# Hash attention and a gated feed-forward on one core: attention steps re-timed, hash bits of both halves together, pair loads two pairs ahead

## The chip, the cores and the metric

The kernel runs on one core of one Trainium2 chip. The metric is the device time of one execution in microseconds (us), as a median over several executions. A profiled execution also gives a span, from the first to the last instruction of the core, and a trace of every instruction. Engines are named as the profile names them: PE (matmul), PEld (its weight loads), DVE (vector), ACT (scalar), POOL, and SP, which here only issues transfers; SPq, ACTq and POOLq are the instruction queues from which transfers are issued.

## The reference

Two blocks in sequence. The attention has 4 batches, 8 heads, 768 positions and head size 64; a query attends to the keys whose six hash bits equal its own. The feed-forward block takes the 3072 x 512 result through 512 x 2048 and 2048 x 512 weights.

```python
q_bits = (np.einsum('bhsd,dk->bhsk', q, proj) > 0).astype(np.int64)   # k_bits likewise
mask = q_bucket[:, :, :, None] == k_bucket[:, :, None, :]
scores = np.where(mask, scale * np.matmul(q, k.transpose(0, 1, 3, 2)), -1000000000.0)
attn = softmax(scores)            # with 1e-9 added to the sum
x = np.matmul(attn, v)            # (B,H,S,D) -> (B*S, H*D)
h = x @ w_in
g = h * erf(softplus(h))
out = g @ w_out
```

The two weight matrices come as 64-bit floats. The kernel turns each into 32-bit floats on the chip, in 16 pieces of 128 x 512 for each matrix.

## The kernel before, in words

**Attention.** Heads go in pairs: 16 pairs, the two heads of a pair in the two halves of the partitions. Each pair has four steps, so there are 64 steps n; pair i has the steps 4i to 4i+3. In the text r is n modulo 4. Steps 4i and 4i+1 serve the first half of the queries (384), 4i+2 and 4i+3 the second; the even step of a half takes the first 384 keys, the odd step the others. The order is written out by hand: inside `tc.manual_schedule()` each engine does its instructions in the order of the program, and waits where an operand is not there. A step consists of

- `scores(n)` on PE: three PSUM tiles `st` (pool tag `big`, three buffers of two banks), first from the bits in bf16, then from q and k in f32, so that pairs without equal bits are pushed far below zero;
- `exponentials(n)` on ACT: three `e` tiles of 128 x 768 (nine tiles in rotation);
- `sum_keys(n)` on DVE: adds the `e` tiles of a half into `sum`; the first addition of a half is L329, the other four are L332;
- `weigh(n)` on PE: `av` from `e` and v, one step later than the scores;
- `divisor(n)` on PE, once for each half, on the step behind its last one: it multiplies `sum` by ones (`z_ps`, L356), which sums over the keys;
- `leave(n)`: ACT copies `av` into `xT` and `z_ps` into `z`.

The hash bits of the next pair are made meanwhile, a quarter in each step: a matmul into a bank of its own (L191), then `take_bits`, on ACT for the bits of q (L197) and on DVE for those of k (L199).

The row of sums `z` is inverted and spread in three parts for each pair: `spread` (SP: `z` to memory as `zd`, and back as `zc`), `invert` (DVE: L398 and L401 on `zc`; SP: `rd<-zc`, then `r<-rd`, which broadcasts it over the partitions), and `normalise` (DVE: L417 multiplies `xT` by `r`). They stand at r = 0, r = 2 and r = 3 of the pair behind. At r = 0, ahead of everything else, SP is also given the six loads of q, k and v of the next pair (`fetch`).

The weights are converted between: `fetch_weights` (POOLq issues the transfer `raw`), `round_weights` part 0 in even steps (ACT: L250, L251; DVE: L254, L262), part 1 in odd ones (DVE: L274, L282, L285; POOL: L293 adds the two parts, `top` and `rest`).

**Feed-forward.** Units of 256 tokens by 512 hidden features; `hidden` (L567) and `project` (L645) on PE, the activation function on ACT and DVE between. Beside it `extremes` reads q and k again to get a bound on the scores, `judge` turns it into a flag, and a second, general form of the attention stands behind a branch on that flag.

The loop of the attention, from the program:

```python
scores(n)
taking = bits(i + 1, r) if i + 1 < NPAIR else None
if 1 <= n <= NS:
    sum_keys(n - 1); weigh(n - 1)
if n < NS:
    exponentials(n)
    if taking: taking()
if 1 <= n <= NS and (n - 1) % 2 == 1:
    divisor(n - 1); leave(n - 1)
```

Of the kernel before, what the change touches and what calls it, by code (L numbers as in the profile page):

```python
# [46 lines left out]
P = 128  # L47
# [16 lines left out]
def kernel(  # L64
# [32 lines left out]
    psum = ctx.enter_context(tc.tile_pool(name="psum", bufs=3, space=PSUM))  # L97
    proj_sb = const.tile([P, P], F32, name="proj_sb")
# [10 lines left out]
    for ab in range(2):  # L109
        for c in range(2):  # L110
            nc.sync.dma_start(
                out=proj_sb[ab * D : ab * D + D, ab * D + c * NBIT : ab * D + (c + 1) * NBIT],
                in_=proj2[ab * D : ab * D + D, ab * NBIT : (ab + 1) * NBIT],
            )
# [69 lines left out]
    def hash_bits(d, r, bitp):  # L184

        what, half = ("q", "q", "k", "k")[r], r % 2
        cols = slice(half * HS, (half + 1) * HS)
        if half == 0:
            d[what + "b"] = bitp.tile([P, S], BF16, name=what + "b", tag=what + "b")
        ps = bank("bits", 1)[:, 0:HS]  # L190
        nc.tensor.matmul(out=ps, lhsT=proj_sb, rhs=d[what][:, cols], start=True, stop=True)  # L191
        return what, cols, ps

    def take_bits(d, what, cols, ps):
        dst = d[what + "b"][:, cols]
        if what == "q":
            nc.scalar.activation(out=dst, in_=ps, func=AF.Sign, scale=2.0**100, bias=sgn[:, 0:1])  # L197
        else:
            nc.vector.tensor_scalar(  # L199
                out=dst,  # L200
                in0=ps,
# [6 lines left out]
    def attention():  # L208
        NS = NPAIR * 4
        with (  # L210
# [4 lines left out]
            tc.tile_pool(name="norm", bufs=1) as norm,  # L215
            tc.tile_pool(name="small", bufs=3) as small,
# [9 lines left out]
            def fetch_weights(n):  # L226
                if n >= len(pieces):
                    return
                if not WIDE:
                    nc.gpsimd.dma_start(out=pieces[n][0], in_=pieces[n][1])  # L230
                else:
                    raws[n] = rawp.tile([P, WP, 2], I32, name="raw", tag="raw")
                    nc.gpsimd.dma_start(
# [3 lines left out]
            def round_weights(n, part):  # L237
# [55 lines left out]
                nc.gpsimd.tensor_tensor(  # L293
# [30 lines left out]
            def sum_keys(n):  # L324
                d = pairs[n // 4]
                es = [etiles[(n * GC + c) % len(etiles)][:, :, 0:HS] for c in range(GC)]
                if n % 2 == 0:
                    d["sum"] = sums.tile([P, 2, HS], F32, name="sum", tag="sum")
                    nc.vector.tensor_tensor(out=d["sum"], in0=es[0], in1=es[1], op=ALU.add)  # L329
                    es = es[2:]  # L330
                for e in es:
                    nc.vector.tensor_tensor(out=d["sum"], in0=d["sum"], in1=e, op=ALU.add)  # L332
# [19 lines left out]
            def divisor(n):  # L352
                d = pairs[n // 4]
                z = d["z_ps"] = bank("z_ps", 1)[:, 0:HS]
                for ab in range(2):
# [3 lines left out]
                        rhs=d["sum"][:, ab, :],  # L359
                        start=True,  # L360
                        stop=True,
                    )

            def leave(n):
# [6 lines left out]
                if half == 0:  # L371
# [8 lines left out]
                    d["z"] = norm.tile([P, S], F32, name="z", tag="z")  # L380
                nc.scalar.copy(out=d["z"][:, cols], in_=d["z_ps"])
# [39 lines left out]
            def bits(i, r):  # L421
                what, cols, ps = hash_bits(pairs[i], r, bitp)
                return lambda: take_bits(pairs[i], what, cols, ps)

            for i in range(2):
                pairs[i] = fetch(i, load)
            for n in range(2):
                fetch_weights(n)
            for r in range(4):
                bits(0, r)()  # L430
            for n in range(NS + 4):
                i, r = divmod(n, 4)
                if n < NS:
                    if r == 0 and i >= 1 and i + 1 < NPAIR:
                        pairs[i + 1] = fetch(i + 1, load)
                    scores(n)
                    taking = bits(i + 1, r) if i + 1 < NPAIR else None
                if 1 <= n <= NS:
                    sum_keys(n - 1)
                    weigh(n - 1)  # L440
                if n < NS:
                    exponentials(n)
                    if taking:
# [339 lines left out]
```

## Time and profile before

| | |
|---|---|
| median of three executions | 1126.29 us (1125.39 to 1129.95) |
| profiled execution: its time / its span | 1128.4 us / 1126.5 us |
| PE busy | 1057.3 us, 94% of the span |
| DVE busy | 809.8 us, 72% |
| ACT busy | 678.0 us, 60% |
| POOL busy | 77.9 us, 7% |
| mean clock granted to PE | 0.983 of full speed |
| first scores (L308) / first feed-forward matmul (L567) | 17.95 us / 441.11 us from the start of the span |

The attention is the stretch between the last two times. In a row of the timeline the columns are start, duration, engine, line, operation and tiles, count, and in brackets the idle time of the engine ahead of it and what ended it. In a row of groups they are busy time and mean duration of one, and behind the last bar the idle time ahead of them with its releasers.

### The profile page before, as it was taken

How to read it: one execution, taken by the hardware profiler on the slowest of the kernel's cores; microseconds unless marked ns; L12 is line 12 of the kernel's file. 1: busy time of each engine (PE TensorE's matmuls, PEld its weight loads, DVE VectorE, ACT ScalarE, POOL GpSimd, SP SyncE). 2: the span in 40 equal slices, each digit the busy share in tenths (PEclk: the TensorE clock that was granted, in tenths of full speed). 3: DMA queues.
4: the chain of work that ended last, by engine and by line, in shares of the span. 5: the costliest groups of instructions: out<-in, count | busy, mean ns of one | idle time of the engine just before them, and what ended most of it. 6: DMA issues, size and time to landing. Idle time of an engine off the chain costs nothing.

```text
span 1126.5 us, 11846 instructions
## 1 busy us (share of the span) xinstructions
PE 1057.3 (94%) x4482; PEld 608.6 (54%) x4482; DVE 809.8 (72%) x962; ACT 678.0 (60%) x785; POOL 77.9 (7%) x68
## 2 busy tenths in 40 slices
PE   5999898999989987989999999999999998999987
PEld 2434333334334334856666666666666665666633
DVE  2767676767777773699787877777777767666692
ACT  3555555555555542597666666666666665666691
POOL 0211111111221120000000000000000000000000
PEclk9999999999999998999999999999999999999999
DMA  7133334434434311100101011111110000000000
GB/s 163 58 95 95 95 95 95 103 96 120 114 99 110 95 53 40 32 29 29 47 28 47 29 47 30 45 42 35 41 47 29 19 9 10 10 10 10 9 19 22
DMA packets 55329, 61.98 MB, mean 55 GB/s; under 512 B 33728, under 2 KB 41920, under 8 KB 55264
## 3 DMA queue, kind: packets, MB, share of 16 engines
q1 hardware_dynamic: 50512, 44.37, 15.6%
q0 software_dynamic: 4608, 16.78, 4.7%
q8 instruction: 37, 0.61, 0.2%
q14 instruction: 28, 0.23, 0.1%
q10 hardware_dynamic: 144, 0.00, 0.0%
HBM read 54.63 MB, written 6.49 MB: 54 GB/s over the span
## 4 chain that ended last, share of the span: by engine, by line
PE 75%; DVE 12%; DMA 8%; issue 2%; ACT 1%; SPq 1%; DVEq 0%
PE h_ps L567 28%; PE o_ps L645 28%; PE st L308 9%; PE av L344 6%; DMA r<-rd 5%; DVE sum L332 5%; PE bits L191 3%; DMA rd<-zc 2%; PE z_ps L356 2%; DVE xT L417 1%; DVE rest L285 1%; DVE top L274 1%; ACT xT L370 1%; SPq L408 1%; DVE unit L282 1%
## 5 line engine op out<-in xcount | busy, mean ns | idle before, releaser
L645 PE MATMUL o_ps<-w_out_sb,h 128*128 128x512 f32 x768 | 338.5, 595 | 7.5 <-DVE h L634 7.5
L567 PE MATMUL h_ps<-xT,w_in_sb 128*128 128x256 f32 x1536 | 342.6, 382 | 0.0
L567 PEld LDWEIGHTS h_ps<-xT,w_in_sb 128*128 128x128 f32 x1536 | 294.5, 192 | 59.1 <-issue 13.4
L645 PEld LDWEIGHTS o_ps<-w_out_sb,h 128*128 128x128 f32 x768 | 146.3, 191 | 175.0 <-issue 166.5
L320 ACT ACTIVATE e<-st 128x768 f32<-128x768 f32 x192 | 141.9, 809 | 92.0 <-PE st L308 89.2
L332 DVE TENSOR_TENSOR sum<-sum,e 128x768 f32<-128x768 f32 x128 | 150.7, 1177 | 9.3 <-DVE sum L332 0.5
L580 ACT COPY h<-h_ps 128x1024 f32<-128x1024 f32 x48 | 48.6, 1013 | 171.8 <-PE h_ps L567 162.8
L308 PE MATMUL st<-q,k 64*128 64x384 f32 x768 | 140.8, 501 | 0.0
L344 PE MATMUL av<-e,v 128*64 128x385 f32 (+1 forms) x768 | 137.9, 495 | 0.0
L626 DVE SCALAR_TENSOR_TENSOR s<-q,s 128x1024 f32<-128x1024 f32 x96 | 111.1, 1220 | 21.8 <-ACT q L625 21.8
L625 ACT ACTIVATE q<-z,cq 128x1024 f32<-128x1024 f32 x96 | 102.3, 1137 | 0.4 <-DVE s L608 0.4
L308 PEld LDWEIGHTS st<-q,k 64*128 64x128 f32 x768 | 75.6, 198 | 41.6 <-issue 6.6
L344 PEld LDWEIGHTS av<-e,v 128*64 128x64 f32 x768 | 49.5, 136 | 80.6 <-issue 71.7
L654 DVE COPY ob<-o_ps 128x512 f32<-128x512 f32 x24 | 16.4, 687 | 79.8 <-PE o_ps L645 79.8
L594 ACT ACTIVATE e<-e 128x1024 f32<-128x1024 f32 x48 | 49.1, 1046 | 35.2 <-DVE e L581 35.2
L356 PE MATMUL z_ps<-sum,ones 128*64 128x384 f32 x128 | 29.9, 545 | 36.8 <-DVE sum L332 36.8
L634 DVE TENSOR_TENSOR h<-h,s 128x1024 f32<-128x1024 f32 x48 | 56.6, 1220 | 7.1 <-ACT s L633 6.7
L598 DVE TENSOR_TENSOR w<-e,w 128x1024 f32<-128x1024 f32 x48 | 58.8, 1225 | 1.7
L608 DVE SCALAR_TENSOR_TENSOR s<-s,w 128x1024 f32<-128x1024 f32 x48 | 58.8, 1225 | 1.6
L605 DVE SCALAR_TENSOR_TENSOR s<-h,s 128x1024 f32<-128x1024 f32 x48 | 58.5, 1219 | 0.0
L626 DVE SCALAR_TENSOR_TENSOR s<-z,s 128x1024 f32<-128x1024 f32 x48 | 56.5, 1220 | 0.0
L667 DVE TENSOR_REDUCE most<-t 128x1 f32<-128x384 f32 x64 | 33.0, 549 | 31.6 <-DMA t<-in_qkT_dram 31.5
(57 smaller groups left out, 821.0 us busy)
## 6 DMA issues: line engine op xcount, KB each, us to landing
t<-in_qkT_dram SPq DMA_DIRECT2D x64, 192.0 KB, 2.4
raw<-in_w_in_dram POOLq DMA_DIRECT2D x16, 512.0 KB, 3.9
raw<-in_w_out_dram POOLq DMA_DIRECT2D x16, 512.0 KB, 3.8
q<-in_qkT_dram SPq DMA_DIRECT2D x32, 192.0 KB, 4.1
k<-in_qkT_dram SPq DMA_DIRECT2D x32, 192.0 KB, 6.9
v<-in_v_dram SPq DMA_DIRECT2D x32, 192.0 KB, 4.5
r<-rd SPq DMA_DIRECT2D x32, 192.0 KB, 3.2
out_dram<-ob SPq DMA_DIRECT2D x24, 256.0 KB, 2.0
```

The lines of the kernel that those rows point to most:

```text
L308: nc.tensor.matmul(out=d["st"][c][:, ab, 0:HS], lhsT=d["k" + src][rows, keys], rhs=d["q" + src][rows, cols], start=(part == 0), stop=(part ...
L320: nc.scalar.activation(out=e[:, :, 0:HS], in_=st[:, :, 0:HS], func=AF.Exp, scale=scale)
L332: nc.vector.tensor_tensor(out=d["sum"], in0=d["sum"], in1=e, op=ALU.add)
L344: nc.tensor.matmul(out=d["av"][rows, 0:w], lhsT=d["v"][:, g * GC + c, rows], rhs=e[:, ab, 0:w], start=(g == 0 and c == 0), stop=(g == 1 an ...
L567: nc.tensor.matmul(out=ps[:, f, :], lhsT=w_in_sb[:, kc, (g * G + f) * P : (g * G + f + 1) * P], rhs=xT[b][:, kc, t0 : t0 + T], start=(kc = ...
L598: nc.vector.tensor_tensor(out=w, in0=e, in1=w, op=ALU.subtract)
L605: nc.vector.scalar_tensor_tensor(out=s, in0=h, scalar=0.0, in1=s, op0=ALU.max, op1=ALU.add)
L608: nc.vector.scalar_tensor_tensor(out=s, in0=s, scalar=S_MAX, in1=w, op0=ALU.min, op1=ALU.add)
L625: nc.scalar.activation(out=q, in_=z, func=AF.Square, bias=cq[:, j : j + 1])
L626: nc.vector.scalar_tensor_tensor(out=s, in0=q, scalar=r, in1=s, op0=ALU.add, op1=ALU.mult)
L634: nc.vector.tensor_tensor(out=d["h"], in0=d["h"], in1=s, op=ALU.mult)
L645: nc.tensor.matmul(out=ps, lhsT=st[t * NG + f // G]["h"][:, f % G, tt * P : (tt + 1) * P], rhs=w_out_sb[:, f, :], start=(f == 0), stop=(f ...
```

## The change

1. `divisor` moves a step later: the one for the half that ended in step n-2 stands at the end of the odd step n, behind `weigh(n-1)`; each half has a `sum` tile of its own in the pair's record, and the copy of `z_ps` moves along. `leave` stays at the even steps.
2. `spread` goes from r = 0 to r = 1, `invert` from r = 2 to r = 3, and `normalise` from r = 3 to r = 1 of the pair after that.
3. The addition that ends a piece of weights moves from POOL to DVE.
4. The bits of both halves are made at once: q at r = 0, k at r = 2, in one tile of the tag `big` instead of the single bank, and taken by one instruction of 768 elements instead of two of 384.
5. The loads of pair i+2 are issued at r = 1 of pair i (before: pair i+1 at r = 0 of pair i).
6. At the start the four small loads of `proj_sb` go to ACT's queue, and the first two pieces of weights to SP's queue, behind the loads of pair 0.
7. Behind step 64 the rest of the last two pairs' work is done in the first three rounds of the feed-forward (`late`), where `normalise(14)`, the last `divisor` and `spread(15)`, `invert(15)` and `normalise(15)` stand behind a `hidden` each.
8. `extremes` takes its tile from the pool of the output tiles (two buffers under the tag `ob`) instead of one of its own.

```diff
-    def hash_bits(d, r, bitp):
-        what, half = ("q", "q", "k", "k")[r], r % 2
-        ps = bank("bits", 1)[:, 0:HS]
-        nc.tensor.matmul(out=ps, lhsT=proj_sb, rhs=d[what][:, cols], start=True, stop=True)
+    def hash_bits(d, what):
+        ps = big("bits")
+        for half in range(2):
+            nc.tensor.matmul(out=ps[:, half, 0:HS], lhsT=proj_sb,
+                rhs=d[what][:, half * HS : (half + 1) * HS], start=True, stop=True)
...
+                queue = nc.sync if n < 2 else nc.gpsimd
...
-                nc.gpsimd.tensor_tensor(
+                nc.vector.tensor_tensor(
                     out=pieces[n][0], in0=top[:, :].bitcast(F32), in1=rest, op=ALU.add
...
+            for n in range(NS + 1):
+                    if r == 1 and i + 2 < NPAIR:
+                        pairs[i + 2] = fetch(i + 2, load)
+                    scores(n)
+                    exponentials(n)
+                    if r % 2 == 0 and i + 1 < NPAIR:
+                        what = "qk"[r // 2]
+                        ps = hash_bits(pairs[i + 1], what)
+                if n >= 1:
+                    sum_keys(n - 1)
+                    weigh(n - 1)
+                if ps is not None:
+                    take_bits(pairs[i + 1], what, ps, bitp)
+                if n >= 1 and n % 2 == 0:
+                    leave(n - 1)
+                if n >= 3 and n % 2 == 1:
+                    divisor(n - 2)
+                round_weights(n // 2, n % 2)
+                if n % 2 == 1:
+                    fetch_weights(n // 2 + 2)
+                if r == 1 and i >= 1:
+                    spread(i - 1)
+                if r == 3 and i >= 1:
+                    invert(i - 1)
+                if r == 1 and i >= 2:
+                    normalise(i - 2)
...
-                t = chk.tile([P, HS], F32, name="t", tag="t")
+                t = outp.tile([P, DM], F32, name="t", tag="ob")[:, 0:HS]
```

How it moves instructions, at three places. In these rows a number behind a tile's name tells its buffers apart.

On DVE, in pair 1 at the end of its last step (r = 3) and the start of pair 2, before: the rows from `take_bits` of k to the last addition of the second half's `sum`.

```order
L199 TENSOR_SCALAR kb_440<-bits_493,kcol_sb_64 128x384
L417 SCALAR_TENSOR_TENSOR xT_0_71<-xT_0_71,ev_279,r_468 128x768
L274 SCALAR_TENSOR_TENSOR top_473<-top_473,keep_472 128x512
L282 TENSOR_SCALAR unit_510<-top_473 128x512
L285 SCALAR_TENSOR_TENSOR rest_511<-raw_327,unit_510 128x512
L332 TENSOR_TENSOR sum_495<-sum_495,e3_125 128x768
L332 TENSOR_TENSOR sum_495<-sum_495,e4_126 128x768
L332 TENSOR_TENSOR sum_495<-sum_495,e5_127 128x768
```

And now, from the last addition of that second half (`sum_484`) on:

```order
L339 TENSOR_TENSOR sum_484<-sum_484,e5_127 128x768
L260 TENSOR_SCALAR top_549<-raw_417 128x512
L268 SCALAR_TENSOR_TENSOR top_549<-raw_417,top_549 128x512
L336 TENSOR_TENSOR sum_581<-e6_128,e7_129 128x768
L339 TENSOR_TENSOR sum_581<-sum_581,e8_130 128x768
L280 SCALAR_TENSOR_TENSOR top_549<-top_549,keep_548 128x512
L288 TENSOR_SCALAR unit_595<-top_549 128x512
L291 SCALAR_TENSOR_TENSOR rest_596<-raw_417,unit_595 128x512
L299 TENSOR_TENSOR w_in_sb_75<-top_549,rest_596 128x512
L426 SCALAR_TENSOR_TENSOR xT_0_77<-xT_0_77,ev_280,r_511 128x768
```

`normalise` (L417, now L426) stood ahead of the last three additions of a second half; now it stands nine rows behind them, and the addition of the weights (L299) has joined DVE.

On PE, the end of step r = 0 of pair 2 before, where the divisor of pair 1's second half stands, with the first rows of the next step:

```order
L191 MATMUL bits_543<-q_518,proj_sb_63 128x384
L344 MATMUL av_498<-e3_125,v_151 64x384 x2
L344 MATMUL av_498<-e4_126,v_151 64x384 x2
L344 MATMUL av_498<-e5_127,v_151 64x384 x2
L356 MATMUL z_ps_558<-sum_495,ones_65 64x384 x2
L308 LDWEIGHTS kb_440
L308 MATMUL st_575<-qb_353,kb_440 128x384
```

Now, the end of step r = 1 of pair 2:

```order
L314 MATMUL st_563<-q_202,k_203 128x384 x2
L314 MATMUL st_564<-q_202,k_203 128x384 x2
L314 MATMUL st_565<-q_202,k_203 128x384 x2
L351 MATMUL av_584<-e6_128,v_204 64x385 x2
L351 MATMUL av_584<-e7_129,v_204 64x385 x2
L351 MATMUL av_584<-e8_130,v_204 64x385 x2
L364 MATMUL z_ps_591<-sum_484,ones_71 64x384 x2
```

The same divisor (of `sum_495` before, of `sum_484` now) has moved a whole step back on PE, and the odd steps have no matmul of bits any more.

On SP, the first transfers of the program, before:

```order
L173 DMA q_140<-in_qkT_dram 64x768
L111 DMA proj_sb_63<-in_proj2_dram 64x6 x4
L173 DMA q_140<-in_qkT_dram 64x768
L173 DMA k_141<-in_qkT_dram 64x768 x2
L178 DMA v_142<-in_v_dram 128x6x64 x2
L173 DMA q_149<-in_qkT_dram 64x768 x2
```

And now:

```order
L175 DMA q_140<-in_qkT_dram 64x768 x2
L175 DMA k_141<-in_qkT_dram 64x768 x2
L180 DMA v_142<-in_v_dram 128x6x64 x2
L239 DMA raw_149<-in_w_in_dram 128x1024
L239 DMA raw_151<-in_w_in_dram 128x1024
L175 DMA q_153<-in_qkT_dram 64x768 x2
```

The four loads of `proj_sb` have left SP's queue (they are the second row of ACT's), and two pieces of weights, which POOL issued first thing, stand between pair 0 and pair 1.

More of the change, by code (lines that the diff above doesn't have):

```diff
@@ L419, in normalise @@
                 )
[L421 to L426, printed above, removed]
+            pairs[0] = fetch(0, load)
             for n in range(2):
                 fetch_weights(n)
-            for r in range(4):
-                bits(0, r)()
-            for n in range(NS + 4):
+            pairs[1] = fetch(1, load)
+            first = [hash_bits(pairs[0], what) for what in "qk"]
@@ L432, in attention @@
+            for what, ps in zip("qk", first):
+                take_bits(pairs[0], what, ps, bitp)
+            for n in range(NS + 1):
                 i, r = divmod(n, 4)
+                ps = None
                 if n < NS:
-                    if r == 0 and i >= 1 and i + 1 < NPAIR:
-                        pairs[i + 1] = fetch(i + 1, load)
+                    if r == 1 and i + 2 < NPAIR:
+                        pairs[i + 2] = fetch(i + 2, load)
                     scores(n)
-                    taking = bits(i + 1, r) if i + 1 < NPAIR else None
@@ L460, in general @@
+        return late
     def general():
@@ L545, in general, with feed_forward @@
                         )
[L549 removed]
+    def feed_forward(check, late):
         with (
```

90 lines of the change are left out of this document (46 added, 44 removed).

## The prediction

> **What bounds the kernel now.** I read first PE's waits in the attention (17.95 to 441.1 us), then the chain that ended last, then the steps on PE's timeline, then the granted clock. The waits, with total, count and longest:
>
> ```profile
> PE z_ps L356 <- DVE sum L332: 36.8, 15, 6.3
> PE bits L191 <- DVE top L274: 2.5, 6, 0.7
> PE bits L191 <- DMA q<-in_qkT_dram: 1.1, 2, 0.9
> ```
>
> PE, busy for nearly the whole span, waits once in each pair but one, for the last additions of `sum`. The chain around one such wait shows why they are late (start, duration, what):
>
> ```profile
> 110.91 1.83 DMA rd<-zc
> ...
> 113.27 4.13 DMA r<-rd
> ...
> 117.51 1.02 DVE xT L417
> ...
> 121.29 1.85 DVE sum L332
> ...
> 123.23 0.97 DVE sum L332
> ```
>
> `normalise` (L417) stands on DVE ahead of the weights' part 1 and of the last three additions, and it waits for two transfers in a row, 1.83 and 4.13 us. The additions end at 124.2; only then the divisor runs, and PE does nothing else meanwhile, since the next scores stand behind it. The second of the three additions takes 1.85 us instead of some 0.96; POOL's addition runs beside it (below).
>
> Steps without such a wait (PE's timeline; a step starts with its scores):
>
> ```profile
> 46.73 0.66 PE L308 MATMUL st<-qb,kb 64*128 64x384 bf16 x6
> 47.23 2.10 PE L308 MATMUL st<-q,k 64*128 64x384 f32 x12
> ...
> 52.20 0.66 PE L308 MATMUL st<-qb,kb 64*128 64x384 bf16 x6
> ...
> 57.55 0.82 PE L356 MATMUL z_ps<-sum,ones 128*64 128x384 f32 x4
> 58.30 0.66 PE L308 MATMUL st<-qb,kb 64*128 64x384 bf16 x6
> 63.76 0.66 PE L308 MATMUL st<-qb,kb 64*128 64x384 bf16 x6
> ```
>
> A step with a divisor is 6.10 us long (52.20 to 58.30), one without 5.47 and 5.46. A pair of pure PE work is 2 x (6.10 + 5.47) = 23.1 us. All 64 steps, without the four quarters of bits (0.91 us each, row at 54.72 below) that the last pair has no successor for, are 16 x 23.14 - 3.6 = 366.6 us; the stretch takes 441.1 - 17.95 = 423.2. So 56.6 us are not work at full speed. 40.4 are the waits above. Much of the rest is in the clock, by stretches of the trace (length, busy time of PE, PEld, DVE, ACT and POOL with counts, then the clock granted to PE):
>
> ```profile
> 125.20:128.60 3.40, 3.40 (x18) 2.00 (x18) 3.23 (x6) 2.58 (x4) 0.00 (x0) 0.53 0.10 25
> ...
> 415.40:418.80 3.40, 3.40 (x16) 2.00 (x14) 3.23 (x5) 2.47 (x4) 0.00 (x0) 0.54 0.10 30
> 435.90:441.10 5.20, 1.47 (x4) 0.32 (x4) 3.37 (x3) 0.00 (x0) 1.70 (x1) 0.50 0.00 2
> 441.10:446.10 5.00, 5.00 (x14) 4.07 (x13) 0.40 (x2) 0.48 (x1) 0.00 (x0) 0.52 0.02 2
> ```
>
> ```profile
> 124.34 0.94 PE L356 MATMUL z_ps<-sum,ones 128*64 128x384 f32 x4 [2.20 <-DVE sum L332]
> ...
> 439.63 1.55 PE L356 MATMUL z_ps<-sum,ones 128*64 128x384 f32 x4 [6.30 <-DVE sum L332]
> ```
>
> The first two stretches are the first and the last of six stretches of 3.4 us at half clock, each right behind a wait for `sum`; each costs 3.4 x 0.47 = 1.6 us, together 9.6. The long wait of 6.3 us at the end is followed by half clock up to 446.1, inside the feed-forward: 5.0 x 0.48 = 2.4 us there, and the last divisor 1.55 us instead of 0.82, 0.7 more.
>
> In the feed-forward, 1126.5 - 441.1 = 685.4 us, PE waits for little:
>
> ```profile
> PE o_ps L645 <- DVE h L634: 7.5, 2, 4.6
> ```
>
> **Divisor, spread, invert and normalise (points 1, 2, 7).** The divisor goes behind a whole step, and `normalise` off the way of the additions it needs. At r = 0 these stand first on DVE and need no transfer. From there to the divisor at the end of r = 1 are a step and a half, 8 us. The wait for `r` moves as well: `invert` stands at r = 3, `normalise` two steps later, 11 us; the chain shows 110.91 to 117.40 for both transfers, 6.5 us. Now q, k and v of another pair are issued on SP just ahead of `spread`, not behind `r`, so `zd` and `zc` may come some us later; they have two steps. I take all of z_ps's waits as gone: -36.8 (between -25, if a third is left, and -36.8). With them go the half clock windows: -9.6, -2.4 and -0.7, sum -12.7 (0 to -12.7; see rival B). The late part costs the feed-forward a `normalise` of 1.02 us in a time in which the first output matmul waits for DVE (4.6 above), and `take(0)` behind a divisor of 0.82: +1 (0 to +2).
>
> By the Trainium skill, "TensorE: Matmul & The Clock Gate", Part 1, PE falls to half its clock after at least one idle window of about 3.4 us. Here the length of the slow stretches agrees (3.40), but the wait before the first is 2.20 us, shorter than that window. Read strictly, the rule would leave six of the seven stretches unexplained; rival B is worked out without it.
>
> **Addition of the weights on DVE (point 3).**
>
> ```profile
> L293 POOL TENSOR_TENSOR w_in_sb<-top,rest 128x512 f32<-128x512 f32 x16 | 30.5, 1904 | 191.6 <-DVE rest L285 191.6
> L332 DVE TENSOR_TENSOR sum<-sum,e x128: 950/959/1851, 23.7 to 438.5; 128x768 f32<-128x768 f32 x128
> L332 DVE TENSOR_TENSOR sum<-sum,e 128x768 f32<-128x768 f32 x128 | 150.7, 1177 | 9.3 <-DVE sum L332 0.5
> L285 DVE SCALAR_TENSOR_TENSOR rest<-raw,unit 128x512 f32<-128x512 uint32 x32 | 22.2, 693 | 1.1
> L199 DVE TENSOR_SCALAR kb<-bits,kcol_sb 128x384 bf16<-128x384 f32 x32 | 21.7, 677 | 39.8 <-PE bits L191 38.2
> 128.60:415.40 286.80, 260.98 (x1484) 112.14 (x1482) 209.43 (x283) 153.71 (x238) 53.30 (x44) 0.98 0.39 98
> ```
>
> An addition of 768 has a median of 0.959 us and a mean of 1.177: eight in a pair lose 8 x 0.218 = 1.7 us, in those beside POOL's. Two new ones of 128 x 512 cost about 0.69 each (nearest row L285, two inputs of the same size; 1.90 on POOL is the other end), 1.4 a pair. DVE gains 0.3 us a pair (between +0.3 and -2.1). It is busy for 73% of 26.4 us a pair (423.2 / 16), 19.3 us, against PE's 23.1: PE stays the bound. Nothing on the path: 0.
>
> **Bits together (point 4).** PE's work is the same, two matmuls of bits at each even step. `take_bits` of k becomes one instruction (0.96 by L332's 768 elements, against 2 x 0.68). New is the buffer: the tile takes turns with `st`. So the bits wait for the exponential that empties the first `st` of their step, and the third `st` of the next step waits until the bits are taken.
>
> ```profile
> 20.43 0.81 ACT L320 ACTIVATE e<-st 128x768 f32<-128x768 f32 x1 [6.53 <-PE st L308]
> ...
> 53.55 2.22 ACT L320 ACTIVATE e<-st 128x768 f32<-128x768 f32 x3 [2.32 <-PE st L308]
> 54.72 0.91 PE L191 MATMUL bits<-k,proj_sb 128*128 128x384 f32 x2
> ```
>
> An exponential is 0.81 us, so the first ends at 54.36, 0.36 before the bits. Behind them `weigh` gives 2.1 us until the next scores, for one instruction of 0.85 to 0.96 us; DVE has the k bits' predecessors done by then at 19 of 23 us. I take 0 (to +0.5 for each of 30, +15).
>
> **Loads (point 5).** The first bits at r = 0 no longer wait for a load issued in their own step: -3.6, both `bits` waits (the row that names `top` is at the same place as the row that names q). Three buffers allow it: the one that is loaded was last read at r = 0 of the step before.
>
> **Start (point 6).**
>
> ```profile
> 0.74 0.58 SPq L173 DMA_DIRECT2D q<-in_qkT_dram  x1
> 1.25 1.22 POOL L233 DMA_DIRECT2D raw<-in_w_in_dram  x2 [0.80 <-POOLq L763]
> 1.38 2.49 SPq L111 DMA_DIRECT2D proj_sb<-in_proj_dram  x4
> 3.91 0.60 SPq L173 DMA_DIRECT2D q<-in_qkT_dram  x1
> 9.34 1.62 PE L191 MATMUL bits<-q,proj_sb 128*128 128x384 f32 x2 [9.34 <-DMA q<-in_qkT_dram]
> 16.37 1.65 PE L191 MATMUL bits<-k,proj_sb 128*128 128x384 f32 x2 [0.77 <-DVE kb L199]
> 17.95 1.14 PE L308 MATMUL st<-qb,kb 64*128 64x384 bf16 x6
> 18.89 3.94 PE L308 MATMUL st<-q,k 64*128 64x384 f32 x12
> proj_sb<-in_proj_dram SPq DMA_DIRECT2D x4, 1.5 KB, 5.6
> ```
>
> The second q goes out at 1.4 instead of 3.91, ahead of the two pieces of weights: it lands by about 5.1 (9.3 less 2.5 for its issue, and less about 1.7 for the traffic). `proj_sb` decides: four issues of 0.62 (2.49 / 4) on ACT's queue behind that of `row` put the last at about 3.0; landing between 2.4 and 5.6 us behind that (5.6 is the median above, among the weights) gives 5.4 to 8.6, and I take 6.5, nearer the low end since the weights come later. Then four bits of 1.62 to 1.65 back to back without the gaps of 0.7 (6.5 us) and one `take_bits` of k with its latencies (1.2): scores at 14.2 instead of 17.95, -3.7 (-1.6 to -4.9). Scores 0 run slow now (1.14 and 3.94, against 0.66 and 2.10 later); with PE unbroken they may come to full speed sooner: -1 (0 to -2.3).
>
> The Trainium skill, "Trainium Kernel Development and Optimization", Key Constraints, says that transfers from SP, ACT and POOL share the same 16 DMA engines, so that another queue saves issue time alone. By it `proj_sb` on ACT's queue would be worth the 2.49 us of SP's issue at most, and the sum 1 us less; no run so far shows the two apart.
>
> **Output tiles shared (point 8).** `extremes` may wait for an output to land, on DVE, in rounds in which PE waits for nothing: 0.
>
> **Sum.** -36.8 - 12.7 - 3.6 - 3.7 - 1 + 1 = -56.8, so a span of 1069.7. Laid out the other way: scores at 14.2, 366.6 of steps, 1.3 of the slow start, 685.4 - 2.4 + 1 = 684.0, together 1066.1; the 3.6 between them is slow work that I can't place. I take 1068. The profiled span (1126.5) lies at the median of the runs (1126.29), so it stands for that too.
>
> **Rivals.** A: as summed, 1068, own range 1059 to 1077. Chance 0.60.
>
> B: the half clock stays, since it follows from something other than these waits. Against A speaks that the gap of 2.2 us is short; for A, that all seven stretches stand behind one. 1068 + 9.6 + 2.4 = 1080. Chance 0.13.
>
> C: PSUM turns. PE waits for the exponential or for the taken bits, 0.5 us at each of 30 places: 1083. For it speaks the margin of 0.36. Chance 0.14.
>
> D: DVE becomes the bound. It waits for `keep` from ACT and for the bits in addition to its 19 us; at 25 us a pair instead of 23.1 it is 16 x 1.9 = 30 more, 1098. Against it the eight us that the divisor has. Chance 0.05.
>
> E, slower or equal: `normalise` waits for `r` longer than its two steps, behind the six loads, and holds the k bits at r = 2 behind it on DVE, and these the third `st` of r = 3. It eats the gain when it costs PE 56.8 / 16 = 3.6 us a pair; with transfers of 6.5 us now, 11 us to run in and some 2 us until k's bits are needed, they would have to take 17. At 4.2 us a pair the time is 1137. Chance 0.08, half of it within 0.5%.
>
> **How the numbers follow.** 0.5%, 5.6 us, is about what a measurement here can tell from no change. Faster are A to D, 0.92; the same 0.04, slower 0.04. The range takes A from 1056 (no cold start at all, an earlier `proj_sb` and a shorter wait before the first output) to C and a bit more, 1086.
>
> **What would show it.** In the profile after: z_ps has no wait for `sum`; scores start every 23.1 us for a pair with odd steps of 5.2 and even ones of 6.3; the clock is full from 20 us to the feed-forward; its first matmul is at 380 to 384 us; L339 has a mean near 0.96; the weights' addition takes 0.69 on DVE; the first bits run at 5.4 to 8.6 us. Wrong it is if PE waits at `bits` or `st` for ACT or DVE, if `normalise` still waits for `r` with the k bits behind it, or if half clock shows without a wait.

## The result, and the profile after

| | before | after | forecast |
|---|---|---|---|
| median | 1127.91 us (1125.39 to 1129.95, four executions) | 1060.62 us (1059.88 to 1060.77, four) | 1068 (1056 to 1086) |
| ratio to before | | 0.9403, 95% interval 0.9379 to 0.9427 | 0.948 |
| profiled execution: time / span | 1128.4 / 1126.5 us | 1059.88 / 1058.1 us | |
| mean clock granted to PE | 0.983 | 0.996 | |
| first scores | 17.95 us | 13.39 us | 14.2 |
| first feed-forward matmul | 441.11 us | 374.08 us | 380 to 384 |

The change makes the kernel 5.97% faster. The span fell by 68.4 us where 58 were forecast. A line of the page of after, busy time by engine:

```profile
PE 1032.3 (98%) x4482; PEld 605.0 (57%) x4482; DVE 798.3 (75%) x978; ACT 674.6 (64%) x769; POOL 16.2 (2%) x34
```

PE was already the bound; now it works for 98% of the span. All of its waits of over half a us in after (total, count, longest):

```profile
PE o_ps L664 <- DVE h L653: 7.4, 2, 4.5
PE bits L189 <- DMA proj_sb<-in_proj_dram: 6.8, 1, 6.8
PE bound L736 <- DVE mk L734: 3.4, 1, 3.4
PE st L314 <- DVE kb L206: 1.2, 1, 1.2
PE st L314 <- ACT qb L204: 0.6, 1, 0.6
```

No wait for `sum` is left. The first and third rows are in the feed-forward, the second and the fourth (1.2) at the start; 0.6, once, is all that PE waits inside the attention. On DVE the wait of `normalise` for its transfers is down to a single one; the first row is of before, the second of after:

```profile
DVE xT L417 <- DMA r<-rd: 41.4, 16, 5.4
DVE xT L426 <- DMA r<-rd: 2.7, 1, 2.7
```

PE's timeline, two whole steps and the start of a third (a step begins with the row `st<-qb,kb`):

```profile
34.13 0.66 PE L314 MATMUL st<-qb,kb 64*128 64x384 bf16 x6
34.62 2.10 PE L314 MATMUL st<-q,k 64*128 64x384 f32 x12
36.65 1.56 PE L189 MATMUL bits<-q,proj_sb 128*128 128x384 f32 x4
38.14 2.15 PE L351 MATMUL av<-e,v 128*64 128x384 f32 x12
40.23 0.66 PE L314 MATMUL st<-qb,kb 64*128 64x384 bf16 x6
40.73 2.10 PE L314 MATMUL st<-q,k 64*128 64x384 f32 x12
42.76 2.16 PE L351 MATMUL av<-e,v 128*64 128x385 f32 x12
44.75 0.81 PE L364 MATMUL z_ps<-sum,ones 128*64 128x384 f32 x4
45.49 0.66 PE L314 MATMUL st<-qb,kb 64*128 64x384 bf16 x6
```

A step with bits takes 6.10 us (34.13 to 40.23), one with a divisor 5.26 (40.23 to 45.49); their starts follow each other without a gap. The two halves of bits stand in a row and take 1.49 us (36.65 to 38.14). The attention and the feed-forward as stretches (length, busy time of PE, PEld, DVE, ACT and POOL with counts, clock granted to PE, share of the DMA engines, GB/s):

```profile
13.39:374.08 360.69, 360.13 (x2164) 163.62 (x2164) 292.46 (x425) 223.03 (x333) 16.03 (x30) 1.00 0.42 108
374.08:1058.10 684.02, 666.73 (x2312) 438.82 (x2310) 503.78 (x532) 449.36 (x434) 0.00 (x0) 0.99 0.09 29
```

In the attention PE is busy for 360.13 of 360.69 us at full clock. The stretch was 423.2 us. What went, by rows of before and after:

| term | us |
|---|---|
| waits of PE inside the attention (40.4 before) | 40.4 |
| half clock behind them (9.6, and 0.7 of the last divisor) | 10.3 |
| scores 0 at full clock (0.66 and 2.10 us, not 1.14 and 3.94) | 2.3 |
| steps shorter: 360.7 of pure work where 366.6 were laid out | 5.9 |
| what the prediction could not place (taken up under "The sum" below) | 3.6 |
| attention in all, 423.2 - 360.7 | 62.5 |
| start, 17.95 - 13.39 | 4.6 |
| feed-forward, 685.4 - 684.0 | 1.4 |

Together 68.5, within 0.1 of the fall of the span. The start, on PE's timeline of after:

```profile
6.76 2.90 PE L189 MATMUL bits<-q,proj_sb 128*128 128x384 f32 x4 [6.76 <-DMA proj_sb<-in_proj_dram]
9.45 2.77 PE L189 MATMUL bits<-k,proj_sb 128*128 128x384 f32 x4
13.39 0.66 PE L314 MATMUL st<-qb,kb 64*128 64x384 bf16 x6 [1.17 <-DVE kb L206]
```

The bits start at 6.76, wait for `proj_sb` as forecast, and by the first scores PE is at full clock. The additions on DVE, as groups (busy, mean ns of one, idle ahead):

```profile
L339 DVE TENSOR_TENSOR sum<-sum,e 128x768 f32<-128x768 f32 x128 | 121.5, 950 | 8.9
L299 DVE TENSOR_TENSOR w_in_sb<-top,rest 128x512 f32<-128x512 f32 x16 | 11.1, 692 | 0.5
```

The additions of `sum` have a mean of 950 ns (1177 before), the weights' addition 692.

### The profile page after: what moved, and what is told of

Read it like the earlier page. It is cut to its first block, busy times and chain, and to the rows that moved or that the text cites. A ratio compares the mean times of both kernels' runs of the same rounds, so it can differ in the third digit from the quotient of the medians.

```text
span 1058.1 us, 11778 instructions
## 1 busy us (share of the span) xinstructions
PE 1032.3 (98%) x4482; PEld 605.0 (57%) x4482; DVE 798.3 (75%) x978; ACT 674.6 (64%) x769; POOL 16.2 (2%) x34
## 4 chain that ended last, share of the span: by engine, by line
PE 94%; DVE 3%; issue 1%; DMA 1%; ACT 1%; ACTq 0%; SPq 0%; DVEq 0%
PE o_ps L664 30%; PE h_ps L586 29%; PE st L314 15%; PE av L351 13%; PE bits L189 5%; PE z_ps L364 2%; DVE s L645 1%; DVE w L617 0%; DVE s L627 0%; DVE h L653 0%; DVE s L624 0%; DMA proj_sb<-in_proj_dram 0%; DVE ob L673 0%; DVE w L614 0%; DMA t<-in_qkT_dram 0%
## 5 line engine op out<-in xcount | busy, mean ns | idle before, releaser
L586 PE MATMUL h_ps<-xT,w_in_sb 128*128 128x256 f32 x1536 | 338.9, 379 | 0.0
L314 PE MATMUL st<-q,k 64*128 64x384 f32 x768 | 134.3, 482 | 0.0
L339 DVE TENSOR_TENSOR sum<-sum,e 128x768 f32<-128x768 f32 x128 | 121.5, 950 | 8.9
L314 PEld LDWEIGHTS st<-q,k 64*128 64x128 f32 x768 | 71.4, 187 | 37.9
L381 ACT COPY xT<-av 128x384 f32<-128x384 f32 x32 | 15.4, 480 | 60.2 <-PE av L351 60.2
```

The lines of the kernel that those rows point to most:

```text
L314: nc.tensor.matmul(out=d["st"][c][:, ab, 0:HS], lhsT=d["k" + src][rows, keys], rhs=d["q" + src][rows, cols], start=(part == 0), stop=(part ...
L339: nc.vector.tensor_tensor(out=d[key], in0=d[key], in1=e, op=ALU.add)
L586: nc.tensor.matmul(out=ps[:, f, :], lhsT=w_in_sb[:, kc, (g * G + f) * P : (g * G + f + 1) * P], rhs=xT[b][:, kc, t0 : t0 + T], start=(kc = ...
```

## The experiments

Unless said, each is the changed kernel with one edit, and its waits are PE's. Ratios are to the kernel before, timed in the same sitting. That kernel scattered from 1120 to 1141 us in these sittings, the others by 1 to 5 us, 7 at most, so versions of the changed kernel are compared by their medians, with 1060.62 us as the mark. The mark itself was not timed again in these sittings: a difference from it of 1 or 2 us counts only where the trace shows where it comes from.

**The divisor at its old place alone** (div_early):

```diff
                 if n >= 1 and n % 2 == 0:
+                    divisor(n - 1)
                     leave(n - 1)
-                if n >= 3 and n % 2 == 1:
-                    divisor(n - 2)
...
-                divisor(NS - 1)
```

> The changed kernel with only the divisor's place undone: it stands again at the end of the even steps, directly behind the half it belongs to; normalise stays late. Theory (PE waited because normalise kept the last additions behind the transfers of r): without normalise ahead of them the additions end some 4.5 us into a step of 6.1, no wait of z_ps for sum over 3 us in total, 1058 to 1064 us. Rival (the divisor needs its extra step): waits of 1 to 2.5 us in each pair return, 16 to 40 us and up to 10 us of half clock, 1077 to 1110.

1067.03 us (1066.40 to 1069.17), ratio 0.9424 [0.9376, 0.9471]. The waits, and PE's timeline at the end of the attention:

```profile
PE z_ps L364 <- DVE sum L339: 4.1, 2, 3.4
```

```profile
378.34 1.55 PE L364 MATMUL z_ps<-sum,ones 128*64 128x384 f32 x4 [3.41 <-DVE sum L339]
```

```profile
377.30:384.10 6.80, 5.76 (x14) 3.78 (x15) 1.91 (x2) 0.86 (x2) 0.00 (x0) 0.51 0.25 61
```

(The last row is a stretch of the trace, columns as above.) Inside the attention 0.7 us of waiting is left: with `normalise` late, the divisor can stay where it was, and the rival is refuted. The time still lies 3 us above the expected range, which left the end of the attention out. The 6.4 us over the mark are the last divisor, which has nothing to stand behind now: 3.4 of waiting and 6.8 x 0.49 = 3.3 of half clock.

**Spread, invert and normalise early, the divisor late** (norm_early). `spread` stays at r = 1, since `z` comes from the late divisor; `invert` is at r = 2 and `normalise` at r = 3 of the next pair, ahead of the weights' work as in the kernel before.

```diff
-                round_weights(n // 2, n % 2)
-                if n % 2 == 1:
-                    fetch_weights(n // 2 + 2)
                 if r == 1 and i >= 1:
                     spread(i - 1)
-                if r == 3 and i >= 1:
+                if r == 2 and i >= 1:
                     invert(i - 1)
-                if r == 1 and i >= 2:
-                    normalise(i - 2)
+                if r == 3 and i >= 1:
+                    normalise(i - 1)
+                round_weights(n // 2, n % 2)
+                if n % 2 == 1:
+                    fetch_weights(n // 2 + 2)
```

> The changed kernel with only invert and normalise moved back, to r = 2 and r = 3 of the pair behind; the divisor stays a step later. DVE waits for r again ahead of the last three additions, 2 to 4 us a pair. Theory (the divisor's place alone takes that in): the additions end 8 us behind the start of r = 0, the divisor stands 11.4 us behind it, no wait of z_ps, 1058 to 1066 us. Rival (DVE's wait reaches PE in another place, as the bits of k come late for the third st of the next step): 1 to 2 us a pair, 1076 to 1095, with waits at st for kb.

1065.94 us (1065.46 to 1066.81), ratio 0.9406 [0.9360, 0.9453]. DVE's wait for the transfers, then PE's waits:

```profile
DVE xT L426 <- DMA r<-rd: 49.8, 15, 4.8
```

```profile
PE st L314 <- DVE kb L206: 4.9, 6, 1.2
...
PE z_ps L364 <- DVE sum L339: 0.9, 1, 0.9
```

DVE stands still for 49.8 us, and of that PE sees little: 0.9 at the divisor, and at most 3.7 more than the start's 1.2 where the k bits are late behind it. (PE also waits 1.5 us for a load in the first pair.)

**Both early** (both_early): the divisor at the even steps, `spread` at r = 0, `invert` at r = 2, `normalise` at r = 3. Of the late part only `invert` and `normalise` of the last pair are left; the other points of the change stay.

```diff
                 if n >= 1 and n % 2 == 0:
+                    divisor(n - 1)
                     leave(n - 1)
-                if n >= 3 and n % 2 == 1:
-                    divisor(n - 2)
+                if r == 0 and i >= 1:
+                    spread(i - 1)
+                if r == 2 and i >= 1:
+                    invert(i - 1)
+                if r == 3 and i >= 1:
+                    normalise(i - 1)
                 round_weights(n // 2, n % 2)
```

> The changed kernel with divisor, spread, invert and normalise all at their old places, the rest of the change kept (late work behind the attention, bits together, weights' addition on DVE, loads two pairs ahead). Theory: the wait for sum is back in each pair, 1.4 to 2.5 us each, 21 to 37 us, and with gaps over some 2 us up to 10 us of half clock: 1085 to 1110. Rival (the gain was in the loads, the bits or the weights' addition): under 1070.

1147.10 us (1142.92 to 1149.22), ratio 1.0114 [1.0058, 1.0170]: 1% slower than the kernel before, and 37 us above the upper end of what was expected. The wait, one divisor on the timeline, two neighbouring stretches there, and a longer one:

```profile
PE z_ps L364 <- DVE sum L339: 56.2, 15, 7.6
```

```profile
120.77 1.55 PE L364 MATMUL z_ps<-sum,ones 128*64 128x384 f32 x4 [2.92 <-DVE sum L339]
```

```profile
117.20:120.60 3.40, 0.65 (x5) 0.00 (x0) 3.19 (x4) 0.00 (x0) 0.53 (x1) 0.99 0.48 148
120.60:124.00 3.40, 3.23 (x14) 1.41 (x16) 2.97 (x5) 1.60 (x4) 0.00 (x0) 0.51 0.04 13
20.00:440.00 420.00, 371.33 (x2050) 164.36 (x2048) 281.52 (x406) 211.16 (x318) 15.97 (x30) 0.93 0.34 89
```

The wait is longer, 3.7 us a pair instead of 2.5, and now half clock follows in nearly every pair (14 times between 20 and 440 us, four of them two stretches long, so 18 stretches of 3.4 us; the kernel before had 6 inside its attention). Why the wait is longer, one pair on the timeline tells. From the start of the step r = 3 (107.06 us) the last addition ends 13.7 us later, at 120.72, as in the kernel before (110.40 and 124.19, 13.8 us). But PE comes to the divisor after 10.8 us (117.85) and not after 11.7 (122.14), since the step r = 3 has no bits now and those of r = 0 wait for nothing. Against the kernel before there are 16 us more waiting and 12 x 1.7 = 20 us more slow work, less the gains at the start and in the bits. The later divisor and the later `normalise` thus cure the same wait:

| | `normalise` late | `normalise` early |
|---|---|---|
| divisor late | 1060.6 | 1065.9 |
| divisor early | 1067.0 | 1147.1 |

Either alone is worth some 80 us, the second on top 5 to 6.

**The kernel before with the late divisor alone** (before_div):

```diff
-                    divisor(n - 1)
                     leave(n - 1)
-                if r == 0 and i >= 1:
+                if n >= 3 and n % 2 == 1 and n - 2 < NS:
+                    divisor(n - 2)
+                if r == 1 and i >= 1:
                     spread(i - 1)
```

> The kernel before with one part of the change alone: the divisor a step later (end of the odd steps), its copy with it, and spread at r = 1; all else as before. Theory: the 14 waits inside the attention go, 30 us, and their half clock, 9.6 us; the wait of 6.3 us at its end and half clock behind it may stay: 1078 to 1092 us, a ratio of 0.956 to 0.968. Rival (it needs normalise late as well): 1100 to 1125.

1087.07 us (1085.74 to 1089.05), ratio 0.9599 [0.9550, 0.9649]. Its waits:

```profile
PE bits L191 <- DMA q<-in_qkT_dram: 13.2, 5, 9.2
PE z_ps L358 <- DVE sum L333: 7.6, 1, 7.6
```

The waits at `sum` inside the attention are gone. What remains is the last one, which `late` takes away in the changed kernel, and waits for loads that stand one pair ahead. So this one part gives 40 to 45 of the 67 us (by the mark's medians and by its own ratio), as expected.

**The weights' addition back on POOL** (pool_add): one line, `nc.vector.tensor_tensor` to `nc.gpsimd.tensor_tensor`.

> The changed kernel with one part undone: the addition that ends a piece of weights is on POOL again. Theory (the addition costs DVE 0.69 us and takes 1.1 us of stretched sums away, and DVE is not the bound): the mean of the sums (L339) rises from 0.95 to about 1.17 us, PE waits for nothing new, 1059 to 1063 us. Rival (DVE's room in the re-timed steps is what the addition's move gave): waits of PE for kb or sum, 1068 to 1085.

1059.39 us (1059.16 to 1060.86), ratio 0.9386 [0.9336, 0.9437].

```profile
L339 DVE TENSOR_TENSOR sum<-sum,e 128x768 f32<-128x768 f32 x128 | 154.4, 1206 | 9.3 <-ACT e L326 0.5
```

The additions of `sum` are slow again (mean 1206 ns, not 950), 33 us of DVE's time, and the kernel is not slower: once PE does not wait for DVE, point 3 is worth nothing that these runs show.

**Bits by quarters** (bits_quarters): a quarter in each step into a bank of its own, each taken by itself.

```diff
-                    if r % 2 == 0 and i + 1 < NPAIR:
-                        what = "qk"[r // 2]
-                        ps = hash_bits(pairs[i + 1], what)
+                    if i + 1 < NPAIR:
+                        ps = hash_quarter(pairs[i + 1], r)
...
-                    take_bits(pairs[i + 1], what, ps, bitp)
+                    take_quarter(pairs[i + 1], *ps, bitp)
```

> The changed kernel with the bits of a next pair in four quarters again, one in each step, in the single bank with the divisor, and taken by four instructions; the first pair as in the changed kernel. In the changed kernel's trace two halves in a row take 1.49 us, in the one before two quarters 2 x 0.84. Theory (the 5.9 us by which the steps came out shorter than laid out are these 0.19 us in 30 steps): pairs of 23.1 us instead of 22.7, 1065 to 1068 us, no new waits. Rival (the shorter steps come from the order, not from the bits): 1059 to 1062.

1065.95 us (1064.37 to 1066.74), ratio 0.9435 [0.9384, 0.9487].

```profile
82.41 0.91 PE L201 MATMUL bits<-q,proj_sb 128*128 128x384 f32 x2
83.25 2.16 PE L379 MATMUL av<-e,v 128*64 128x384 f32 x12
```

A quarter takes 0.84 us (82.41 to 83.25), so four take 3.36 where two halves in a row take 2 x 1.49 = 2.98. Fifteen pairs make 5.7. The attention of this kernel, from 13.23 us on, is some 5 us longer than that of after, which has 0.6 us of waiting for bits that this one has not.

**Loads one pair ahead again** (load_one), at r = 0, the rest as changed:

```diff
-                    if r == 1 and i + 2 < NPAIR:
-                        pairs[i + 2] = fetch(i + 2, load)
+                    if r == 0 and i >= 1 and i + 1 < NPAIR:
+                        pairs[i + 1] = fetch(i + 1, load)
```

> The changed kernel with the loads of a pair issued one pair ahead again, at the start of r = 0. Theory: there they stand on SP behind r<-rd, which the re-timed invert now issues some 5 us into r = 0; q lands some 7 us behind the place at which PE wants it for the bits; PE waits 5 to 8 us in 14 pairs, with half clock behind it: 1140 to 1190 us. Rival (SP runs far enough ahead, as in the kernel before, where the wait was 1.1 us in all): under 1075.

1202.79 us (1199.62 to 1204.67), ratio 1.0651 [1.0590, 1.0711].

```profile
PE bits L189 <- DMA q<-in_qkT_dram: 109.4, 14, 9.6
```

```profile
96.81 1.19 SPq L175 DMA_DIRECT2D q<-in_qkT_dram  x2
101.40 2.90 PE L189 MATMUL bits<-q,proj_sb 128*128 128x384 f32 x4 [8.05 <-DMA q<-in_qkT_dram]
```

Thirteen of the waits are 7.8 to 9.6 us long, one at the start is 1.5; 5 to 8 were expected. Half clock follows each of the thirteen (the bits above take 2.90 instead of 1.56 us). Both were put too low, and the time lies 13 us above the expected range. On SP the loads stand behind `r<-rd`, which waits for `invert` at r = 3: it goes out at 95.62 here, the load of q behind it at 96.81, while PE came to the bits at 93.35. In the kernel before the loads stood behind `r<-rd` too, but `invert` was a step earlier, and q went out (at 113.95) before its step began (115.85).

**The start as before** (start_old): `proj_sb` on SP's queue, both pairs' loads ahead of the weights, these on POOL's queue.

```diff
-            nc.scalar.dma_start(
+            nc.sync.dma_start(
...
-                queue = nc.sync if n < 2 else nc.gpsimd
+                queue = nc.gpsimd
...
-            pairs[0] = fetch(0, load)
+            for i in range(2):
+                pairs[i] = fetch(i, load)
```

> The changed kernel with the start undone: the loads of proj_sb on SP's queue, the first two pieces of weights on POOL's queue at once, both first pairs ahead of them. Theory: the first bits run at 9.3 us instead of 6.76 as in the kernel before, all else alike: 1062.5 to 1064.5 us. Rival (what decides is the number of bytes, not their order): no difference, 1060 to 1061.5.

1062.61 us (1061.82 to 1064.00), ratio 0.9415 [0.9364, 0.9465].

```profile
9.28 2.90 PE L189 MATMUL bits<-q,proj_sb 128*128 128x384 f32 x4 [9.28 <-DMA q<-in_qkT_dram]
...
15.46 0.66 PE L314 MATMUL st<-qb,kb 64*128 64x384 bf16 x6 [1.17 <-DVE kb L206]
```

Scores at 15.46 instead of 13.39, and 2.0 us in the time. The other 2.5 us of the start (17.95 to 15.46) come from the bits in a row. The new start brings the first bits from 9.28 to 6.76, 2.52 us. The Trainium skill, "Trainium Kernel Development and Optimization", Key Constraints, says that another queue saves only issue time. SP's issue of `proj_sb` took 2.49 us, which fits, but this run moves the weights' first pieces and the second pair's loads as well, and no run shows `proj_sb`'s move alone.

**Both early, with the wait filled** (early_filled): both_early with two matmuls ahead of each second half's divisor, whose result nothing uses.

```diff
                 z = bank("z_ps", 1)[:, 0:HS]
+                if half == 1:
+                    for _ in range(2):
+                        nc.tensor.matmul(
+                            out=z, lhsT=proj_sb, rhs=d["k"][:, 0:HS], start=True, stop=True
+                        )
```

> The kernel of both_early (1147 us) with work added: ahead of the divisor of each second half PE does two more matmuls of 128 x 384 that nobody needs (about 1.7 us, into the bank that the divisor then overwrites). In both_early the gaps in front of that divisor are some 2.9 us, and every stretch at half clock lies behind an aligned stretch of 3.41 us with more than 2.0 us of idle PE; stretches with 1.88 or less had none behind them. Theory (the clock goes by idle time within one such stretch): gaps of 1.2 to 1.5, no half clock inside the attention, and although PE does 27 us more the time falls to 1105 to 1120 us. Rival (the half clock comes from something else, or the chain of transfers alone sets the pair): 1143 us or more.

1123.57 us (1122.04 to 1128.92, ten executions), ratio 0.9957 [0.9920, 0.9993]: 23.5 us faster than both_early by the medians, some 18 by the two ratios, although it does 16 x 1.56 us of needless work. Waits, timeline and stretches:

```profile
PE z_ps L369 <- DVE sum L339: 31.0, 15, 6.3
```

```profile
115.15 1.56 PE L365 MATMUL z_ps<-k,proj_sb 128*128 128x384 f32 x4
117.97 0.87 PE L369 MATMUL z_ps<-sum,ones 128*64 128x384 f32 x4 [1.26 <-DVE sum L339]
```

```profile
194.49:197.90 3.41, 1.25 (x6) 0.20 (x4) 3.17 (x5) 0.00 (x0) 0.00 (x0) 0.98 0.49 154
197.90:201.30 3.40, 3.40 (x16) 1.94 (x16) 3.04 (x5) 2.96 (x5) 0.00 (x0) 0.51 0.03 4
20.00:440.00 420.00, 389.00 (x2213) 175.50 (x2210) 293.07 (x422) 215.10 (x328) 15.96 (x30) 0.99 0.34 90
```

The needless work took the place of waiting (56.2 to 31.0) and the gaps fell to 1.3 us. One stretch of half clock is left ahead of the attention's end (the second row); the clock from 20 to 440 us is 0.99 instead of 0.93. Some 15 stretches fewer by 1.67 us are 25 us. The order on the other engines is that of both_early; what the edit took away is idle time of PE, and the half clock went with it. The rival that it would stay is refuted. The time came out a little above the range. One thing in the expectation does not hold: in both_early the second of two slow stretches in a row follows a stretch with little idle time (last section).

**The late part ahead of the feed-forward** (late_off):

```diff
         late = attention()
-        feed_forward(judge, late)
+        for k in range(3):
+            late(k)
+        feed_forward(judge, None)
```

> The changed kernel with one part undone: what is left of the last two pairs stands behind the attention, ahead of the first hidden, instead of between the first three rounds of the feed-forward. Theory: PE waits for the last sums 1 to 3.4 us (3.4 with the divisor early), with one or two stretches at half clock, and DVE waits for zc and r while the first h is ready: 1064 to 1070 us. Rival (the feed-forward's first output matmul waits anyway and takes it in): 1060 to 1062.

1062.54 us (1061.38 to 1063.02), ratio 0.9373 [0.9316, 0.9431]. The last divisor waits, at full clock:

```profile
376.73 0.87 PE L364 MATMUL z_ps<-sum,ones 128*64 128x384 f32 x4 [2.39 <-DVE sum L339]
```

1.9 us more than the mark, between the expected range and the rival's: the wait of 2.39 had no half clock behind it here.

**A version that beats both** (better). After's remaining waits are the output's for DVE (7.4) and the flag's for `mk` (3.4). `extremes` now runs in rounds 4 to 19 of the feed-forward instead of 1 to 16, and `judge` is cut in two: the exchange of the maxima, and a round later the flag's matmul.

```diff
-                if check and 1 <= p:
-                    for m in range(4 * p - 4, 4 * p):
+                if check and 4 <= p:
+                    for m in range(4 * p - 16, 4 * p - 12):
...
-                if check and p == NPAIR + 2:
-                    check()
+                if check and p == NPAIR + 4:
+                    check[0]()
+                if check and p == NPAIR + 5:
+                    check[1]()
```

> The changed kernel with two edits in the feed-forward: extremes runs in rounds 4 to 19 instead of 1 to 16, so that the first three rounds, in which the first output matmul waits 4.5 us for DVE, have none of its reductions and waits for loads; and the flag's matmul comes a round behind the exchange of the maxima for which PE waited 3.4 us. Theory: the wait of 4.5 us falls by 3 to 4.5 us, with its stretch of half clock (1.7 us), and the 3.4 us go: 1050 to 1055 us. Rival (the first output matmul is held by the chain through ACT and not by DVE's extra work; the other wait moves with the flag): 1058 to 1061.

1050.76 us (1048.10 to 1051.95, six executions), ratio 0.9267 [0.9223, 0.9311].

```profile
PE o_ps L664 <- DVE h L653: 3.5, 2, 2.9
```

9.9 us under the mark: the flag's wait (3.4) is gone, the output's fell by 3.9, and one stretch of half clock (1.7) went with it. The two edits were not timed apart.

## Why the prediction was right, point by point

The time was 7.4 us below the forecast, inside the own range of rival A (1059 to 1077).

**Divisor and normalise, -36.8 and -12.7.** Right in both terms and in their cause. Every wait for `sum` and every stretch of half clock inside the attention left together, and early_filled brought the clock back without touching the order of DVE. Rival B is out. What the prediction did not see is that the two moves are one cure given twice: it took them as one term, as if both were needed. The half clock's own condition it left open; the experiments narrow it down (last section).

**The addition on DVE, 0.** Right: 692 ns, a mean of 950 for `sum`, and no change in the time that counts with POOL (1059.39).

**Bits together, 0 (to +15).** This is the mis-sized term. "PE's work is the same" was wrong: two halves in a row take 1.49 us, not 2 x 0.84 = 1.68, which is 0.19 x 30 = 5.7 us of the 5.9 by which the steps are shorter. The bounds left a gain out for no reason. So the even steps take 6.10 us and not 6.3, a pair 22.7 and not 23.1, and the feed-forward begins at 374.08, ahead of the 380 to 384 forecast. Rival C, PSUM, cost 0.6 us in all.

**Loads, -3.6.** Right as a step from the kernel before: the waits are gone. What the prediction did not see is that point 2 cannot do without this point. With `invert` at its new place the loads two pairs ahead are worth 142 us (1202.79 - 1060.62), since they would else stand behind the later `r<-rd`.

**Start, -3.7 and -1.** `proj_sb` decided, at 6.76 (6.5 taken). The scores came 0.8 earlier than laid out, as the four bits took 5.46 us (6.76 to 12.22) and not 6.5, and they ran at full clock from the first, 2.3 instead of 1.

**The feed-forward, 684.0 forecast, 684.02 measured.** The half clock at its start (2.4) is gone, and two stretches of it are left, as many as before behind that place; by difference the late part costs the 1 us that was taken. That it all agrees to the last digit is luck. late_off shows what the late part saves at the end of the attention, 1.9 us. Output tiles shared: the waits at `o_ps` are 7.4 us (7.5 before), so 0 holds.

**The sum.** The forecast lay 7 us too high, mostly for the term of the bits. Laid out the second way it was 1066.1. Less 5.9 for the steps, 0.8 for the start and 1.3 for the slow scores it gives 1058.1, the span measured. The 3.6 that could not be placed belong to the waits. In the kernel before, a step that holds a wait is longer by more than the wait: the one from 89.94 to 98.83 us has 2.52 us of waits and 6.37 besides, where the one from 40.63 to 46.73 without a wait takes 6.10. At some 0.2 us in each of 14 such steps this makes about 3 us; the rest is that the six slow stretches cost 3.41 x 0.5 = 1.7 us each and not 1.6. Why a stop of PE costs more than the wait is open.

**Rivals D and E.** DVE is 81% busy in the attention (292.46 of 360.69) and PE waits 0.6 us for bits; `normalise` waits for its transfers once, 2.7 us.

## What to carry to other kernels

Where one engine is the bound and waits a little in each round, look for the instruction that another engine puts ahead of the operand although it waits for a transfer, and move either that instruction or the reader: one is enough, and the second move pays little. Price a moved load against the new order of its queue, not the old one. Count a wait of PE with the slow stretch that follows it, and ask of each gap if it is long enough to bring one.

## What the runs showed of the hardware

PE's half clock comes in stretches of 3.41 us on a fixed grid (in the kernel before 125.2, 152.5, 179.8, 207.1: 27.3 us apart, 8 x 3.41; the one at 415.4 comes 85 x 3.41 behind the first). Out of full clock such a stretch follows when the stretch of the grid ahead of it is idle for more than some 2.0 us; it need not be idle throughout. Of the kernel before, three pieces of its trace:

```profile
121.76:125.17 3.41, 1.21 (x8) 0.23 (x4) 3.27 (x4) 0.48 (x1) 1.07 (x2) 0.97 0.45 135
125.17:128.60 3.43, 3.43 (x18) 2.00 (x18) 3.26 (x6) 2.58 (x4) 0.00 (x0) 0.53 0.11 27
...
384.63:388.04 3.41, 2.15 (x13) 0.77 (x12) 3.20 (x4) 1.17 (x3) 2.42 (x2) 1.00 0.58 86
388.04:391.45 3.41, 2.43 (x18) 1.34 (x20) 3.27 (x5) 1.50 (x3) 0.00 (x0) 1.00 0.40 156
391.45:394.87 3.42, 3.42 (x20) 1.29 (x18) 3.25 (x6) 2.86 (x5) 1.12 (x1) 1.00 0.03 2
...
94.47:97.88 3.41, 1.34 (x10) 0.31 (x6) 3.20 (x4) 0.48 (x1) 2.05 (x2) 1.00 0.19 28
```

In the first, PE is busy for 1.21 of 3.41 us, idle for 2.20, and the next stretch runs at 0.53. In the second a gap of 2.23 us lies across a border, 1.26 on one side and 0.98 on the other, and the clock stays at 1.00. In the third 2.07 us of idle time have no effect (the clock of the stretch behind it is 1.00). Over the attention of before, both_early and early_filled, all stretches at full clock with 2.13 us or more had half clock behind them, those with 1.95 or less none, and between 1.98 and 2.07 both occur. (These figures move by some 0.1 us with where the borders of the grid are laid.) A stretch that is itself slow can be followed by another with less idle time ahead. In both_early the one from 148.00 to 151.40 was busy for 2.81 of 3.40 us, and the next was still slow:

```profile
151.31:154.72 3.41, 3.41 (x12) 1.39 (x10) 2.44 (x5) 2.66 (x4) 0.00 (x0) 0.51 0.25 57
```

Why is open. One place in the feed-forward does not fit: around the flag's matmul stretches with no more than 1.8 us of idle time had half clock behind them in the kernel before and in late_off, while 1.7 us had none in after. The same wait can thus cost 1.7 us more or nothing, by where it falls on the grid: 2.39 us cost nothing in late_off, where some 2.0 to 2.1 of it lay in one stretch; 2.16 us in one stretch did in early_filled. The Trainium skill, "TensorE: Matmul & The Clock Gate", Part 1, asks for an idle window of about 3.4 us; the length of the stretches agrees, but half clock out of full clock came here after some 2.0 us of idle time in a stretch.

Two groups of matmuls on the same weights in a row cost 0.19 us less than apart. By these rows each group of bits has some 0.19 us of its own beside its matmuls; what it is was not tested.
